# Hash attention with a feed-forward block on one core: the scaled sum of values written into the accumulators' banks ahead of the value products in 11 of 24 halves, banks dealt in the order of making, order remade

## The chip, the core and the metric

The kernel runs on one core of a Trainium2 chip. The metric is the device time of one execution in microseconds; lower is better. Three runs of the kernel before took 295.97, 294.70 and 294.19 us, a median of 294.7 us. Five engines work side by side: PE (matrix products; PEld is its loading of weights), DVE (vector), ACT (scalar, activation functions), POOL, and SP, which issues DMA. Each engine takes its own instructions strictly in the order in which the program writes them and waits for the others by semaphores.

## The reference

`q`, `k` and `v` are 4 batches x 8 heads x 768 tokens x 64, `proj` is 64 x 6, the block is 512 wide with 2048 hidden columns.

```python
q_bits = (einsum('bhsd,dk->bhsk', q, proj) > 0);  k_bits likewise      # 6 bits each
mask   = (bucket of q_bits)[..., :, None] == (bucket of k_bits)[..., None, :]
scores = where(mask, q @ k.T / sqrt(64), -1e9)
attn   = softmax(scores) @ v                        # x = heads side by side, (4, 768, 512)
xn     = (x - mean) / sqrt(var + 1e-6) * g_ln
out    = x + relu(xn @ w_ch1) @ w_ch2
```

A query whose bucket holds no key sees -1e9 everywhere, so that its softmax is uniform and its row is the plain mean of the 768 values. The kernel gets this row by adding 2^-100 times the sum of the values to the numerators, and 2^-100 x 768 to the denominator: beside a single matching key the addend is nothing, without one it is all there is.

## The kernel before

**Units and halves.** The work is cut into 12 units `u` of 256 queries (three to a batch, `u // 3` is the batch), and each unit into two halves `(u, g)` of four heads. A half goes through these steps:

- `S` (L606, PE), six words, one for each block of 128 keys: the scores of four heads, each head in its own 32 rows of the array. Three rounds of products go into the same place: the bucket bits `G` (which push keys of another bucket far down), and the two halves of `q` times `k`.
- `E` (L623, ACT): exp of one score tile of 128 x 1024, from PSUM to bf16 in SBUF. From unit 3 on a half has six tiles in two threes ("trios"): a trio is filled by three `S` words, and emptied by three `E`.
- `A` (L634, PE), six words of eight products: exp tiles times values. `vaug` is the values with a column of ones, so that numerators and denominators (4 heads x 65 columns, for two query tiles: 2 x 260) gather in one accumulator tile `acc` of two banks.
- `na` (L646, DVE): `y = vsB * 2^-100 + acc`, where `vsB` holds, in every partition, the batch's sums of values (made by `su`, `sp` and `sc`, L527 or L525) and in column 64 the constant 768. `acc` is free after it.
- `nb` (L653 to L661, DVE): the reciprocal of the denominators and two products `x = y * rc` that also give the row sums for the norm.

Then the unit's norm (`mn`, `sv`, `rs`, `ce`; POOL, ACT and DVE), a DMA transpose (`fl`), the first feed-forward product and the second. The first product of units 1 to 3 and 11 is plain (`F`, relu `R`, L725, L733, L735). That of units 4 to 10 is made by seven half-size products `M` (L791), whose results are combined out of PSUM by `V` (copy, L800 on ACT or L802 on DVE), `U` (add, L809, DVE), `Q` (relu, L813 or L815) and `ru` (relu, L821 or L823). The second product is made the same way with seven products `P` (L880), combined into `x` by `Y` (L885). `w1s` and `sw` make sums of the weights once, and `tu`, `CA`, `hm`, `bt`, `mw`, `mr`, `cv`, `su` prepare queries, keys, buckets and values of the next batch, all in between.

**PSUM.** Pool `pp` has three places of two banks each. Score tiles and accumulators (and two wide tiles of unit 10) take turns in them; pool `f` has two places of one bank for all else. Which place a tile gets is written in `SLOTS`: the n-th tile made in `pp` takes place `pp[n]`, so the digit decides whose `E` (or `na`) it must wait for.

**Order.** `ORDER` is a list of 1498 words, written out. A word names the step, the engine (t is PE, v DVE, a ACT, p POOL, s SP) and its numbers: `E.a.7.0.1.2` is the exp of half (7, 0), trio 1, tile 2. Every engine executes its words in this order.

Of the kernel before, what the change touches and what calls it, by code (L numbers as in the profile page):

```python
# [10 lines left out]
AOP = mybir.AluOpType  # L11
# [34 lines left out]
A.t.2.1.2.1 na.v.2.1 nb.v.2.1 mw.s.1.1 LX.s.2.0.0 D.t.0.1.0 wg.a.0 ce.v.1.1 fl.s.1.1 ce.v.1.0 fl.s.1.0  # L46
S.t.3.0.0 N.a.3.0.0 sw.v.2.1 cv.a.1.0.2 CA.a.1.1.0 CA.v.1.1.1 S.t.3.0.1 E.a.3.0.0.1 S.t.3.0.2 E.a.3.0.0.0
E.a.3.0.0.2 LX.s.2.0.1 mr.s.1.1.2 mr.s.1.1.0 nc.v.2.1 mr.s.1.1.3 D.t.0.0.2 D.t.0.1.1 D.t.0.1.2 D.t.0.1.3
D.t.0.0.3 tu.v.2.0.0.0 mr.s.1.1.1 sw.v.3.0 ag.v.2.0 tu.v.2.0.0.2 ag.v.2.1 S.t.3.0.3 S.t.3.0.4 Z.v.0.0
N.a.3.0.1 S.t.3.0.5 cv.a.1.0.0 lv.s.1.4.2 Z.v.0.1 E.a.3.0.1.1 F.t.1.1 R.a.1.1 wg.v.2 F.t.1.7 R.v.1.7  # L50
E.a.3.0.1.0 F.t.1.0 E.a.3.0.1.2 rs.p.2 R.a.1.0 lv.s.1.4.1 F.t.1.6 lv.s.2.0.1 lv.s.1.4.0 tu.v.2.0.0.1 ce.v.2.1
S.t.3.1.0 N.a.3.1.0 R.a.1.6 S.t.3.1.1 S.t.3.1.2 ce.v.2.0 w1s.v.1.1 tu.v.2.0.1.1 E.a.3.1.0.2 F.t.1.4
tu.v.2.0.0.3 R.a.1.4 sw.v.2.0 sw.v.1.1 F.t.1.2 A.t.3.0.0.1 R.a.1.2 A.t.3.0.0.2 LX.s.2.1.1 E.a.3.1.0.0 sw.v.4.0
sw.v.1.0 A.t.3.0.1.2 A.t.3.0.1.1 sp.t.1.0 A.t.3.0.0.0 A.t.3.0.1.0 F.t.1.5 E.a.3.1.0.1 cv.a.1.4.0 R.a.1.5
sc.v.1.0 na.v.3.0 su.v.1.4 F.t.1.3 S.t.3.1.3 N.a.3.1.1 S.t.3.1.4 E.a.3.1.1.1 S.t.3.1.5 E.a.3.1.1.0 E.a.3.1.1.2
fl.s.2.1 fl.s.2.0 R.v.1.3 tu.v.2.0.1.3 P.t.1.2 Y.v.1.2 F.t.2.1 R.a.2.1 P.t.1.1 S.t.4.0.0 ss.v.1.1 N.a.4.0.0
S.t.4.0.1 E.a.4.0.0.1 S.t.4.0.2 sw.v.4.1 tu.v.2.0.1.2 O.s.0.2 Y.v.1.1 ss.v.1.2 ss.v.1.4 P.t.1.5 Y.v.1.5
P.t.1.6 cv.a.1.4.2 E.a.4.0.0.2 tu.v.2.0.1.0 ss.v.1.3 CA.a.2.0.1 Y.v.1.6 lv.s.2.0.3 P.t.1.3 lv.s.2.0.0 Y.v.1.3
E.a.4.0.0.0 O.s.0.3 lv.s.2.0.2 lv.s.2.4.2 lv.s.2.4.1 CA.a.2.0.0 A.t.3.1.1.1 A.t.3.1.1.2 w1s.v.2.1 A.t.3.1.1.0
A.t.3.1.0.0 sp.t.1.4 sc.v.1.4 nb.v.3.0 P.t.1.7 A.t.3.1.0.1 A.t.3.1.0.2 Y.v.1.7 na.v.3.1 F.t.2.6 R.v.2.6  # L60
S.t.4.0.3 nb.v.3.1 N.a.4.0.1 S.t.4.0.4 E.a.4.0.1.1 LX.s.2.1.0 S.t.4.0.5 E.a.4.0.1.0 hm.t.2.0 bt.v.2.0 mn.p.3
sv.a.3.1 sv.a.3.0 P.t.1.4 Y.v.1.4 F.t.2.3 R.a.2.3 tu.v.2.1.1.2 su.v.2.0 F.t.2.4 E.a.4.0.1.2 F.t.2.2 rs.p.3
on.p.2 R.a.2.4 w1s.v.4.1 ce.v.3.0 ce.v.3.1 S.t.4.1.0 S.t.4.1.1 N.a.4.1.0 R.a.2.2 S.t.4.1.2 mw.s.2.0 lv.s.2.4.3
lv.s.2.4.0 F.t.2.5 E.a.4.1.0.1 F.t.2.7 R.a.2.5 tu.v.2.1.0.0 tu.v.2.1.0.2 tu.v.2.1.1.3 w1s.v.1.0 tu.v.2.1.1.1
A.t.4.0.0.0 A.t.4.0.1.1 A.t.4.0.1.0 A.t.4.0.1.2 E.a.4.1.0.0 fl.s.3.0 A.t.4.0.0.1 A.t.4.0.0.2 na.v.4.0 F.t.2.0
R.v.2.0 E.a.4.1.0.2 R.a.2.7 S.t.5.0.0 N.a.5.0.0 S.t.5.0.1 E.a.5.0.0.1 cv.a.2.0.0 S.t.5.0.2 E.a.5.0.0.2
ss.v.2.1 ss.v.2.2 E.a.5.0.0.0 P.t.2.2 Y.v.2.2 tu.v.2.1.0.3 P.t.2.1 fl.s.3.1 F.t.3.6 R.a.3.6 Y.v.2.1 P.t.2.6
S.t.4.1.3 N.a.4.1.1 S.t.4.1.4 O.s.0.1 E.a.4.1.1.1 S.t.4.1.5 ss.v.2.4 tu.v.2.1.1.0 P.t.2.5 tu.v.2.1.0.1 Y.v.2.6
ss.v.2.3 Y.v.2.5 P.t.2.7 su.v.2.4 mr.s.2.0.3 O.s.1.1 P.t.2.3 O.s.0.0 O.s.1.0 O.s.1.3 Y.v.2.3 E.a.4.1.1.0
A.t.4.1.1.0 A.t.4.1.0.2 E.a.4.1.1.2 A.t.4.1.0.0 nb.v.4.0 A.t.4.1.1.1 A.t.4.1.1.2 A.t.4.1.0.1 na.v.4.1  # L70
mr.s.2.0.2 Y.v.2.7 F.t.3.1 S.t.5.0.3 S.t.5.0.4 N.a.5.0.1 S.t.5.0.5 R.a.3.1 nb.v.4.1 w1s.v.3.1 mr.s.2.0.1
E.a.5.0.1.2 P.t.2.4 Y.v.2.4 F.t.3.4 E.a.5.0.1.1 E.a.5.0.1.0 CA.v.2.1.1 hm.t.2.1 CA.v.2.1.0 cv.v.2.4.0
w1s.v.3.0 bt.v.2.1 cv.v.2.0.2 R.a.3.4 S.t.5.1.0 N.a.5.1.0 mn.p.4 sv.a.4.1 sv.a.4.0 S.t.5.1.1 S.t.5.1.2 rs.p.4
E.a.5.1.0.2 F.t.3.7 R.a.3.7 LX.s.3.0.1 LX.s.3.0.0 tu.v.3.0.0.2 F.t.3.2 A.t.5.0.1.1 A.t.5.0.0.2 A.t.5.0.0.1
E.a.5.1.0.1 R.a.3.2 tu.v.3.0.1.1 mr.s.2.0.0 A.t.5.0.1.2 A.t.5.0.0.0 ce.v.4.0 fl.s.4.0 tu.v.3.0.1.0
tu.v.3.0.0.1 A.t.5.0.1.0 ce.v.4.1 na.v.5.0 tu.v.3.0.1.3 mw.s.2.1 O.s.1.2 F.t.3.5 R.a.3.5 F.t.3.3 F.t.3.0
tu.v.3.0.0.0 R.v.3.0 E.a.5.1.0.0 tu.v.3.0.0.3 R.a.3.3 S.t.5.1.3 N.a.5.1.1 S.t.5.1.4 E.a.5.1.1.1 ss.v.3.1
S.t.5.1.5 E.a.5.1.1.2 E.a.5.1.1.0 P.t.3.2 Y.v.3.2 fl.s.4.1 w1s.v.2.0 ss.v.3.2 P.t.3.1 lv.s.3.0.0 P.t.3.5
O.s.2.1 Y.v.3.5 Y.v.3.1 S.t.6.0.0 N.a.6.0.0 S.t.6.0.1 cv.a.2.4.2 S.t.6.0.2 E.a.6.0.0.2 E.a.6.0.0.0 P.t.3.6
ss.v.3.4 E.a.6.0.0.1 CA.v.3.0.0 Y.v.3.6 P.t.3.3 mr.s.2.1.0 tu.v.3.0.1.2 ss.v.3.3 nb.v.5.0 Y.v.3.3 CA.a.3.0.1  # L80
A.t.5.1.1.2 A.t.5.1.1.1 A.t.5.1.0.0 A.t.5.1.1.0 A.t.5.1.0.2 A.t.5.1.0.1 P.t.3.7 na.v.5.1 nb.v.5.1 mn.p.5
Y.v.3.7 hm.t.3.0 bt.v.3.0 S.t.6.0.3 N.a.6.0.1 S.t.6.0.4 E.a.6.0.1.1 bs.v.4.1 bs.v.4.3 bs.v.4.2 S.t.6.0.5
mr.s.2.1.3 E.a.6.0.1.2 O.s.2.0 sp.t.2.0 sc.v.2.0 mr.s.2.1.2 LX.s.3.1.0 mr.s.2.1.1 P.t.3.4 Y.v.3.4 M.t.4.1.0
V.v.4.1.0 E.a.6.0.1.0 M.t.4.2.0 U.v.4.1.0 mw.s.3.0 S.t.6.1.0 O.s.3.0 N.a.6.1.0 w1s.v.4.0 M.t.4.6.0 sv.a.5.1
# [77 lines left out]
TYPES = "222222333333333333333333"  # L162

WIDE = {10}
SUMS = 3

SLOTS = dict(
    B="000000",
# [15 lines left out]
    vnat="01010101",  # L184
    vsB="0101",
    vsum="000",
    x="012301320132",
    xnT="010101010101",
)

@with_exitstack
def kernel(
# [16 lines left out]
    P = 128  # L209
# [80 lines left out]
    def vsB(b):  # L290
        return sb(f"vsB{b}", [P, H, D + 1], F32, "vsB", 2)
# [652 lines left out]
```

## Time and profile before

| | |
|---|---|
| median of three runs | 294.7 us |
| the profiled execution: its time, and its span from the first to the last instruction | 293.72 us, 292.0 us |
| PE busy | 280.4 us, 96% of the span, 4924 products |
| DVE busy | 244.8 us, 84%, 587 instructions |
| ACT busy | 228.9 us, 78%, 285 instructions |
| POOL busy | 32.9 us, 11% |
| TensorE clock granted | 1.000 |
| exp `E` on ACT | 144 of 1112 ns |
| `na` on DVE | 24 of 690 ns |

The profile gives for each engine the time in which it executed something. Products on PE are pipelined and their ends are modelled, so "busy" is not "at its peak" there. In a list of groups a row reads: line, engine, operation, tile written <- tiles read, shapes, count | busy us, mean ns of one | idle time of the engine just before them, and what ended it. In a list of waits a row reads: who <- for whom: us in total, times, longest us. Times in a timeline are us from the start of the span.

### The profile page before, as it was taken

What the parts mean: (1) busy time and instruction counts of PE and PEld (TensorE: products, weight loads), DVE (VectorE), ACT (ScalarE), POOL (GpSimd) and SP (SyncE); (2) the same over time, 40 slices, a digit from 0 to 9 for tenths busy, and PEclk for the clock granted to TensorE, in tenths of its full rate; (3) what the DMA queues carried; (4) which work ended last, traced back from release to release, by engine and by line L of the source; (5) the groups of instructions that cost most, each with busy time, mean ns of one, the idle gap of its engine ahead of it and who ended that gap; (6) DMA issues with size and microseconds to landing.
All of it is one profiled execution on the core that took longest, in us unless ns stands there. A gap on an engine that the chain in (4) does not pass through costs nothing.

```text
span 292.0 us, 11314 instructions
## 1 busy us (share of the span) xinstructions
PE 280.4 (96%) x4924; PEld 228.0 (78%) x4927; DVE 244.8 (84%) x587; ACT 228.9 (78%) x285; POOL 32.9 (11%) x83
## 2 busy tenths in 40 slices
PE   8998999999999999999998999899999999999993
PEld 5777767558887886877886878698788789998882
DVE  5758899899998989898997899797997997998552
ACT  4889999999999859879847989898897896664240
POOL 4560500110003002001000102000101011010000
PEclk9999999999999999999999999999999999999999
DMA  6999999268752560444942012500042202003233
GB/s 205 362 293 270 217 278 173 58 203 225 203 159 75 135 225 2 111 146 106 205 140 60 4 38 57 114 11 2 12 101 56 57 3 55 24 0 56 53 93 91
DMA packets 31059, 34.15 MB, mean 117 GB/s; under 512 B 15521, under 2 KB 27809, under 8 KB 31010
## 3 DMA queue, kind: packets, MB, share of 16 engines
q1 hardware_dynamic: 25938, 28.72, 35.4%
q0 software_dynamic: 4224, 4.19, 8.7%
q8 instruction: 38, 0.62, 0.9%
q10 hardware_dynamic: 848, 0.53, 0.7%
q14 instruction: 11, 0.09, 0.1%
HBM read 27.86 MB, written 6.88 MB: 119 GB/s over the span
## 4 chain that ended last, share of the span: by engine, by line
PE 84%; DVE 7%; ACT 6%; issue 1%; DVEq 0%; ACTq 0%
PE sc L606 17%; PE X L880 12%; PE acc L634 11%; PE f L725 10%; PE Ma L791 7%; PE Yb L880 6%; ACT E L623 4%; PE Ya L880 3%; PE Me L791 3%; PE hp L550 3%; PE hf L418 3%; PE f L828 2%; PE Mb L791 2%; PE warm L388 1%; DVE T L329 1%
## 5 line engine op out<-in xcount | busy, mean ns | idle before, releaser
L623 ACT ACTIVATE E<-sc,bias_sb 128x1024 bf16<-128x1024 f32 x144 | 152.2, 1112 | 17.8 <-PE sc L606 17.2
L606 PE MATMUL sc<-qb,kb 32*128 32x256 bf16 x1152 | 52.4, 267 | 0.0
L606 PE MATMUL sc<-G 6*128 6x256 bf16 (+1 forms) x576 | 43.0, 272 | 3.2 <-ACT E L623 3.1
L634 PE MATMUL acc<-vaug,E 128*128 128x65 bf16 x1152 | 43.1, 193 | 0.4 <-ACT E L623 0.4
L634 PEld LDWEIGHTS <-E 128*128 128x128 bf16 x1152 | 40.5, 97 | 2.1 <-issue 1.0
L725 PE MATMUL f<-xnT,w_sb 128*128 128x256 bf16 x320 | 38.8, 273 | 0.4 <-ACT hb L733 0.2
L880 PEld LDWEIGHTS <-hb 128*128 128x128 bf16 x352 | 33.0, 98 | 7.3 <-issue 3.1
L725 PEld LDWEIGHTS <-w_sb 128*128 128x128 bf16 x320 | 30.2, 98 | 5.4 <-issue 2.1
L606 PEld LDWEIGHTS <-kb 32*128 32x128 bf16 x1152 | 30.6, 93 | 1.2
L606 PEld LDWEIGHTS <-G 6*128 6x128 bf16 (+1 forms) x576 | 17.4, 91 | 17.2 <-issue 12.4
L733 ACT ACTIVATE hb<-f 128x512 bf16<-128x512 f32 x33 | 19.6, 599 | 13.5 <-PE f L725 10.5
L880 PEld LDWEIGHTS <-S 128*128 128x128 bf16 x264 | 25.2, 98 | 4.3 <-issue 1.1
L329 DVE STREAM_TRANSPOSE T<-X 128x384 f32<-128x384 f32 (+2 forms) x52 | 26.6, 539 | 0.0
L885 DVE TENSOR_TENSOR x<-X,x 128x256 f32<-128x256 f32 x44 | 18.3, 418 | 5.8 <-PE X L880 5.6
L880 PE MATMUL Yb<-w_sb,S 128*128 128x256 bf16 x176 | 22.8, 273 | 0.0
L791 PEld LDWEIGHTS <-w_sb 128*128 128x128 bf16 x336 | 20.2, 97 | 3.0 <-issue 2.8
L880 PE MATMUL X<-wt,hb 128*128 128x256 bf16 x168 | 21.8, 273 | 0.0
L791 PEld LDWEIGHTS <-Wx 128*128 128x128 bf16 x336 | 19.6, 98 | 2.3 <-issue 2.1
L646 DVE SCALAR_TENSOR_TENSOR y<-vsB,acc 128x520 f32<-128x520 f32 x24 | 16.6, 690 | 5.0 <-PE acc L634 4.8
L669 POOL TENSOR_TENSOR rw<-rw 128x2 f32<-128x2 f32 x9 | 2.1, 237 | 139.1 <-DVE x L659 139.1
L791 PE MATMUL Ma<-bs,Wx 128*128 128x128 bf16 x192 | 14.7, 219 | 0.0
L659 DVE SCALAR_TENSOR_TENSOR x<-y,rc 128x256 f32<-128x256 f32 x36 | 13.9, 422 | 0.6
(134 smaller groups left out, 441.4 us busy)
## 6 DMA issues: line engine op xcount, KB each, us to landing
out_dram<-x SPq DMA_DIRECT2D x45, 128.0 KB
X<-in_k_dram SPq DMA_DIRECT2D x7, 768.0 KB
vn<-in_v_dram SPq DMA_DIRECT2D x24, 192.0 KB
X<-in_q_dram SPq DMA_DIRECT2D x6, 768.0 KB
w_sb<-in_moe_w_ch_dram POOLq DMA_DIRECT2D x8, 512.0 KB, 12.5
vn<-in_v_dram SPq DMA_DIRECT2D x2, 768.0 KB
X<-in_q_dram SPq DMA_DIRECT2D x2, 512.0 KB
Bd<-B SPq DMA_DIRECT2D x6, 96.0 KB
```

The source lines that it names most:

```text
L329: nc.vector.transpose(d[:, j], s[:, j, kj0 : kj0 + n])
L418: nc.tensor.matmul(hf(g, t, kp)[:, :256], pfull[:, j], tp(g, t, kp)[:, j], start=(j == 0), stop=(j == 1))
L606: m = nc.tensor.matmul(sc(u, g, a, p)[:, bank, 256 * half : 256 * half + 256], lh, rh, start=(rep == 0), stop=(rep == 2), skip_group_check ...
L623: nc.scalar.activation(Ep(u, g, a, p), sc(u, g, a, p), AF.Exp, scale=EXP_SCALE, bias=bias_sb)
L634: nc.tensor.matmul(acc[:, qt, (D + 1) * i : (D + 1) * (i + 1)], Ep(u, g, a, p)[:, bank, 256 * half + P * qt : 256 * half + P * qt + P], va ...
L646: nc.vector.scalar_tensor_tensor(yt(u, g), vs, EPS_ROW, made[f"acc{u}_{g}"][:, :, :A], op0=AOP.mult, op1=AOP.add,)
L659: nc.vector.scalar_tensor_tensor(xo[:, t], a[:, t, :, 0:D], 1.0, rc[:, t].to_broadcast([P, 4, D]), op0=AOP.mult, op1=AOP.mult, accum_out=r ...
L725: nc.tensor.matmul(f1[:, n].rearrange("p (t x) -> p t x", t=2), w1_sb[:, dt, P * nt : P * nt + P], xnT(u)[:, :, dt], start=(dt == 0), stop ...
L733: nc.scalar.activation(hb(u)[:, 2 * p : 2 * p + 2], f1, AF.Relu)
L791: nc.tensor.matmul(m[:, n], lh(kt)[:, P * nt : P * nt + P], rh[:, kt], start=(first and n == 0 and kt == 0), stop=(kt == 1), skip_group_ch ...
L880: nc.tensor.matmul(f2, lh[:, n], rh[:, n], start=(first and n == 0), stop=(n == 7), skip_group_check=True)
L885: nc.vector.tensor_tensor(x, made[f"{prod(u, k)}{u}"], x, op=AOP.add)
```

## The change

Three things are changed together.

1. In 11 halves, (4,0), (4,1), (5,0), (5,1), (7,1), (8,1), (9,0), (10,0), (10,1), (11,0) and (11,1), a new step `pa` copies the scaled sum of values into the accumulator's two banks before the first `A` of the half; all 48 value products then add to it. `na` is gone there, and `nb` reads numerators and denominators straight from `acc` in PSUM instead of from `y`. Nine `pa` stand on ACT, two (unit 11) on DVE. The set `LATE` names the 13 halves that keep `na`. So that nothing need be scaled at that point, `vsB` is scaled by 2^-100 when it is made, for batches 1 to 3 (`sc`, `on`). The score products now open each bank once (`opened`), where each 256 columns opened it before.
2. The places in `pp`, `f`, `E`, `X` and `x` are dealt anew, in the order in which the tiles are made. In `pp`, of the 128 tiles made from unit 3 on, 119 took the place that stands first in `ORDER` to be freed; now 125 do.
3. `ORDER` is remade from its 300th word on (PE is changed from its 112th word on). It has the same number of words. Besides `na` and `pa`, 47 words change their engine between ACT and DVE.

```diff
-A.t.2.1.2.1 na.v.2.1 nb.v.2.1 mw.s.1.1 LX.s.2.0.0 D.t.0.1.0 wg.a.0 ce.v.1.1 fl.s.1.1 ce.v.1.0 fl.s.1.0
+A.t.2.1.2.1 na.v.2.1 nb.v.2.1 mw.s.1.1 D.t.0.0.2 D.t.0.1.0 wg.a.0 cv.a.1.0.0 lv.s.1.4.0 LX.s.2.0.0 S.t.3.0.0
...
+LATE = {(u, g) for u in range(3) for g in range(2)} | set([(3, 0), (3, 1), (6, 0), (6, 1), (9, 1), (7, 0), (8, 0)])
...
-    pp="012120212021102012012012010120120201021021021012021002010212102012102121012011022021210021010201201020120102102120102101200210201210202110210212012021120101201201202102021",
+    pp="012120212021102012012012010120120201021021021012021001202102102012102121020121202102021210201210210212012102120120101202010210102012021012010212102021201210212012100210120",
...
     def on(eng, b):
         nc.gpsimd.memset(vaug(b)[:, :, :, D : D + 1], 1.0)
-        nc.gpsimd.memset(vsB(b)[:, :, D : D + 1], float(S))
+        nc.gpsimd.memset(vsB(b)[:, :, D : D + 1], float(S) * (EPS_ROW if b else 1.0))
...
     def scp(eng, b, hs):
...
+        elif eng is nc.scalar:
+            nc.scalar.activation(dst, src, AF.Copy, scale=EPS_ROW)
+        else:
+            eng.tensor_scalar(dst, src, EPS_ROW, None, op0=AOP.mult)
...
+                fresh = (u, g, a, p, bank) not in opened
+                opened.add((u, g, a, p, bank))
                 m = nc.tensor.matmul(
                     sc(u, g, a, p)[:, bank, 256 * half : 256 * half + 256], lh, rh,
-                    start=(rep == 0), stop=(rep == 2), skip_group_check=True,
+                    start=fresh, stop=(rep == 2), skip_group_check=True,
                 )
...
+    def pa(eng, u, g):
+        acc = ps(f"acc{u}_{g}", [P, 2, 512], "pp")[:, :, :A]
+        vs = vsB(u // 3)[:, 4 * g : 4 * g + 4].rearrange("p h e -> p (h e)").unsqueeze(1).to_broadcast([P, 2, A])
+        if eng is nc.scalar:
+            nc.scalar.copy(acc, vs)
+        else:
+            eng.tensor_copy(acc, vs)
...
-        first, last = begun[u, g] == 1, begun[u, g] == 6
+        first, last = begun[u, g] == 1 and (u, g) in LATE, begun[u, g] == 6
...
-            yt(u, g), vs, EPS_ROW, made[f"acc{u}_{g}"][:, :, :A], op0=AOP.mult, op1=AOP.add,
+            yt(u, g), vs, 1.0 if u > 2 else EPS_ROW, made[f"acc{u}_{g}"][:, :, :A], op0=AOP.mult, op1=AOP.add,
...
-        a = yt(u, g).rearrange("p t (h e) -> p t h e", e=D + 1)
+        a = (yt(u, g) if (u, g) in LATE else made[f"acc{u}_{g}"][:, :, :A]).rearrange("p t (h e) -> p t h e", e=D + 1)
```

Two places show how the order moves. The first is ACT's queue from the second trio of half (8,1) to the next three exp of half (9,0); the names are the tile with its unit, half, trio and place in the trio (`E8_111` is half (8,1), trio 1, tile 1), `hb6` is the hidden layer of unit 6, `V651` a copy for its `U`. Before:

```order
L623 ACTIVATE E8_111_4509<-sc8_111_4446,bias_sb_66 128x1024
L623 ACTIVATE E8_110_4512<-sc8_110_4457,bias_sb_66 128x1024
L623 ACTIVATE E8_112_4522<-sc8_112_4443,bias_sb_66 128x1024
L813 ACTIVATE hb6_4425<-Ma60_4334 128x4x128
L623 ACTIVATE E9_000_4564<-sc9_000_4524,bias_sb_66 128x1024
L623 ACTIVATE E9_002_4581<-sc9_002_4551,bias_sb_66 128x1024
L800 COPY V651_4631<-Me61_4622 128x512
L623 ACTIVATE E9_001_4641<-sc9_001_4527,bias_sb_66 128x1024
```

Now, with the copy into `acc8_1` (`pa`, L638) among them:

```order
L630 ACTIVATE E8_111_4493<-sc8_111_4436,bias_sb_66 128x1024
L630 ACTIVATE E8_112_4495<-sc8_112_4447,bias_sb_66 128x1024
L630 ACTIVATE E8_110_4499<-sc8_110_4433,bias_sb_66 128x1024
L828 ACTIVATE hb6_4414<-Ma60_4352 128x4x128
L630 ACTIVATE E9_001_4559<-sc9_001_4512,bias_sb_66 128x1024
L638 COPY acc8_1_4561<-vsB2_2649 128x2x260
L630 ACTIVATE E9_002_4587<-sc9_002_4509,bias_sb_66 128x1024
L815 COPY V651_4616<-Me61_4607 128x512
L630 ACTIVATE E9_000_4661<-sc9_000_4536,bias_sb_66 128x1024
```

The three exp of half (8,1) come in another order, and so do those of (9,0). The first `S` word of half (9,0) fills tiles `sc9_000` and `sc9_001` before; by the digits of `pp` they took the places of `sc8_112` (the third of the three exp above) and of `sc8_110` (the second). Now the first `S` word fills `sc9_002` and `sc9_001`, in the places of `sc8_111` and `sc8_112`, the first and the second exp. The same holds at half (7,1): its first `S` word took the places of the third and second exp of the trio before it, `E7_010` and `E7_012`; now it takes those of the first and second, `E7_011` and `E7_010`. At both places one or two `M` stand on PE between this `S` word and the next one, which needs the third.

The second place is DVE's queue around the end of half (8,1): `acc8_1` is its accumulator, `rc81` the reciprocals, `hb6`, `S61`, `bs7` and `x6` belong to the feed-forward parts of units 6 and 7. Before:

```order
L646 SCALAR_TENSOR_TENSOR y81_4685<-vsB2_2195,acc8_1_4603 128x520
L809 TENSOR_TENSOR hb6_4425<-Me61_4622,V661_4620 128x4x128
L823 TENSOR_SCALAR hb6_4425<-hb6_4425 128x8x128 x2
L865 TENSOR_TENSOR S61_4698<-hb6_4425 128x1024
L767 TENSOR_TENSOR bs7_4737<-xnT7_4578 128x256
L885 TENSOR_TENSOR x6_3606<-Ya6_4753,x6_3606 128x256
```

Now:

```order
L838 TENSOR_SCALAR hb6_4414<-hb6_4414 128x8x128
L668 RECIPROCAL rc81_4694<-acc8_1_4561 128x8
L674 SCALAR_TENSOR_TENSOR x8_4421,rw8_4422<-acc8_1_4561,rc81_4694 128x256 x2
L824 TENSOR_TENSOR hb6_4414<-Me61_4607,V661_4605 128x4x128
L838 TENSOR_SCALAR hb6_4414<-hb6_4414 128x8x128
L880 TENSOR_TENSOR S61_4700<-hb6_4414 128x1024
L900 TENSOR_TENSOR x6_3646<-Ya6_4744,x6_3646 128x256
```

Before, one instruction freed the accumulator, and the reciprocal and the two products of this half came twelve rows later, after most of the `Y` of unit 6. Now these three free the accumulator, and stand ahead of the `U`, `ru` and first sum that unit 6 still needs.

More of the change, by code (lines that the diff above doesn't have):

```diff
@@ L50 @@
[L50 to L64, printed above, removed]
@@ L70 @@
[L70 to L84, printed above, removed]
@@ L186 @@
     vsum="000",
-    x="012301320132",
+    x="012301230123",
     xnT="010101010101",
```

208 lines of the change are left out of this document (119 added, 89 removed).

## The prediction

> **What bounds the kernel now.** I read the busy times first, then stretches of the time line, then the waits, and last the two places where PE stood still longest.
>
> ```profile
> span 292.0 us, 11314 instructions
> PE 280.4 (96%) x4924; PEld 228.0 (78%) x4927; DVE 244.8 (84%) x587; ACT 228.9 (78%) x285; POOL 32.9 (11%) x83
> PE 84%; DVE 7%; ACT 6%; issue 1%; DVEq 0%; ACTq 0%
> ```
>
> PE is busy for 96% of the span and carries 84% of the chain that ended last. The change neither removes nor adds a product: PE has 4924 before and after. So only PE's standing still can be won, and only lengthening it can lose. The changed part of PE's program begins at 57.9 us and the last product ends at 287.4 us; I cut that time where the fifth unit's second half ends its first trio (113 us) and where unit 9 begins (186 us). Columns: length, then busy us of PE, PEld, DVE, ACT, POOL, each with its instructions, the clock, the DMA share and GB/s.
>
> ```profile
> 57.90:113.00 55.10, 54.99 (x873) 42.47 (x875) 50.35 (x113) 48.97 (x59) 4.20 (x10) 1.00 0.58 164
> 113.00:186.00 73.00, 71.33 (x1364) 58.32 (x1361) 65.91 (x155) 60.43 (x78) 5.76 (x16) 1.00 0.37 92
> 186.00:248.00 62.00, 60.69 (x1180) 52.33 (x1176) 52.62 (x125) 51.67 (x66) 4.41 (x12) 1.00 0.18 42
> 248.00:287.40 39.40, 39.09 (x504) 35.26 (x500) 29.90 (x72) 17.58 (x29) 1.40 (x4) 1.00 0.19 44
> sum 229.50, PE 226.09 PEld 188.37 DVE 198.78 ACT 178.65 POOL 15.76; mean PE 56.52 PEld 47.09 DVE 49.69 ACT 44.66 POOL 3.94
> ```
>
> Over these 229.5 us PE stands still for 229.50 - 226.09 = 3.4 us, and 1.7 us of that lies in the stretch from 113 to 186. Visible idle time is therefore a small prize. DVE has 55.10 - 50.35 = 4.8 us left in the first stretch, 7.1 in the second, 9.4 in the third. Whom PE waited for in these 229.5 us:
>
> ```profile
> PE sc L606 <- ACT E L623: 2.4, 2, 1.3
> PE acc L634 <- ACT E L623: 0.3, 1, 0.3
> ACT E L623 <- PE sc L606: 14.0, 25, 1.7
> DVE y L646 <- PE acc L634: 2.9, 5, 1.2
> ```
>
> Two waits of score products for an exp make 2.4 of the 3.4 us. In the other direction ACT waits 14.0 us for scores, 25 times: ACT is seldom late. PE's and ACT's rows at the two places, 155 and 185 us:
>
> ```profile
> 156.10 0.61 PE L791 MATMUL Me<-bs,Wx 128*128 128x128 bf16 x8
> 157.97 0.29 PE L606 MATMUL sc<-G 6*128 6x256 bf16 x4 [1.27 <-ACT E L623]
> 154.80 3.12 ACT L623 ACTIVATE E<-sc,bias_sb 128x1024 bf16<-128x1024 f32 x3 [0.20 <-PE sc L606]
> 185.73 0.61 PE L791 MATMUL Ma<-bs,w_sb 128*128 128x128 bf16 x8
> 187.43 0.29 PE L606 MATMUL sc<-G 6*128 6x256 bf16 x4 [1.09 <-ACT E L623]
> 229.43 0.63 PE L606 MATMUL sc<-G 6*128 6x256 bf16 x4
> 184.25 3.12 ACT L623 ACTIVATE E<-sc,bias_sb 128x1024 bf16<-128x1024 f32 x3 [0.22 <-PE sc L606]
> ```
>
> Both times three exp run in a row, and PE goes on only behind the third: 154.80 + 3.12 = 157.92, then 157.97. The reader is to see which exp it is. The waiting word is the first `S` of (7,1), and of (9,0); its two tiles had the banks of the third and of the second exp. At 229.43 us, the first `S` of (11,0), where the banks were those of the first and second, no wait is seen, only 0.63 us in place of 0.29 for the four products.
>
> **The change, part by part.** *Banks.* At these two places the first `S` word now gets the banks of the first and second exp. It can go on one exp earlier, 3.12 / 3 = 1.04 us, and the third exp is needed only by a later `S`, with one or two `M` ahead of it. Of 1.27 and 1.09 us that wins 1.0 each, **-2.0 us**; the bounds are 0 (something else is late) and -2.4.
>
> *Work moved.* The rows that give the durations:
>
> ```profile
> L646 DVE SCALAR_TENSOR_TENSOR y<-vsB,acc 128x520 f32<-128x520 f32 x24 | 16.6, 690 | 5.0 <-PE acc L634 4.8
> L659 DVE SCALAR_TENSOR_TENSOR x<-y,rc 128x256 f32<-128x256 f32 x36 | 13.9, 422 | 0.6
> L653 DVE RECIPROCAL rc<-y 128x8 f32<-128x8 f32 x24 | 4.7, 194 | 0.3
> L885 DVE TENSOR_TENSOR x<-X,x 128x256 f32<-128x256 f32 x44 | 18.3, 418 | 5.8 <-PE X L880 5.6
> L733 ACT ACTIVATE hb<-f 128x512 bf16<-128x512 f32 x33 | 19.6, 599 | 13.5 <-PE f L725 10.5 <-PE sc L606 2.9
> L477 ACT ACTIVATE w_sb<-w_sb,gT 128x512 bf16<-128x512 bf16 x4 | 2.5, 716 | 0.0
> L802 DVE COPY V<-Ma 128x512 f32<-128x512 f32 x11 | 7.6, 689 | 2.4 <-PE Ma L791 2.4
> L498 ACT CAST vaug<-vn 128x768 bf16<-128x768 f32 x10 | 8.3, 833 | 1.0 <-DMA G<-Bd 0.6 <-PE sc L606 0.4
> L500 DVE CAST vaug<-vn 128x768 bf16<-128x768 f32 x3 | 1.7, 554 | 0.0
> L336 ACT ACTIVATE kb<-T 128x1536 bf16<-128x1536 f32 x3 | 4.5, 1486 | 0.0
> L340 DVE CAST kb<-T 128x1536 bf16<-128x1536 f32 x3 | 2.9, 951 | 0.0
> L821 ACT ACTIVATE hb<-hb 128x1024 bf16<-128x1024 bf16 x6 | 6.3, 1056 | 0.8 <-DVE hb L809 0.4 <-PE sc L606 0.4
> L823 DVE TENSOR_SCALAR hb<-hb 128x1024 bf16<-128x1024 bf16 x15 | 6.1, 422 | 0.2
> L754 DVE TENSOR_TENSOR Wx<-w_sb 128x1024 bf16<-128x1024 bf16 x4 | 2.7, 676 | 0.0
> L693 DVE TENSOR_SCALAR xc<-x,rw,rs 128x512 bf16<-128x512 f32 x18 | 9.4, 533 | 0.4 <-POOL rs L702 0.4
> L329 DVE STREAM_TRANSPOSE T<-X 128x384 f32<-128x384 f32 x44 | 23.4, 556 | 0.0
> ```
>
> DVE loses 11 `na`, 11 x 0.690 = 7.6 us. It gains two `pa` (1.4 at 0.69), a net four evictions of 128x512 (`V`, `R`, `Q`: 4 x 0.689 = 2.8), a net two `CA`, the casts of `q` and `k` (three come, one goes: 2 x 0.951 = 1.9), four casts of values (2.2) and one relu (0.4), and gives up two copies of 128x256 (0.8). The sum is -7.6 + 1.4 + 2.8 + 1.9 + 2.2 + 0.4 - 0.8 = **+0.3 us**: DVE's load stays.
>
> ACT gains nine `pa`. None is in the trace, and none reads SBUF and writes PSUM. The bounds by the nearest 512-wide rows are 599 ns (from PSUM) and 716 ns (inside SBUF); I take 650 ns, between them, 5.9 us in all. It loses a net four evictions (4 x 0.60 = 2.4), two `CA` (3.0), four casts (3.3) and one relu (1.1), and gains the two small copies, under 0.6 each. That is about **-3 us** on an engine with 14 us of waiting: it pays nothing by itself, but lets exp be on time. By the Trainium skill, "ScalarE: Activation LUTs", section "Step-by-step: what each stage is for", an activation that writes to PSUM is the faster one; by that sentence the nine copies would cost 599 ns or less, 5.4 us, which changes the total by nothing, since ACT's 3 us have no price.
>
> *Where DVE's work lies.* Between the same two marks, 113 and 186 us, DVE's words change: three `na` and a `CA` net in (-2.1 + 1.0), three evictions more (2.1), two casts of values (1.1), one `nb` more (0.194 + 2 x 0.422 = 1.0), two weight sums `w1s` (1.4), less one norm product and one transpose (1.1). That is **+3.4 us** in the stretch, and as much less outside it. DVE would be busy 65.9 + 3.4 = 69.3 of 73 us. What it costs is bounded by 0 (all goes into the 7.1 us in which DVE waits) and +3.4 (none does). In the stretch before, DVE was at 91% and PE stood still for 0.1 us, so that load at this level costs next to nothing; I take **+0.5**.
>
> *The accumulator's release.* `acc` was free one instruction after the last `A` (0.690 us); now after the reciprocal and two products, 1.04 us. `nb` reads PSUM now. The row with one operand in PSUM (`x<-X,x`, 418 ns) and the row from SBUF alone (422 ns) agree, so I count no extra. The Trainium skill speaks against that: "Perfetto Trace Analysis", section "Optimizing Scalar/DVE Operations", has about 125 ns of access for DVE on PSUM and 60 on SBUF; by it 33 instructions would add an estimated 2.1 us to DVE. The two rows of this trace show no such step. The bank comes 0.35 us later in 11 halves; at three, (4,1), (8,1) and (9,0), only one `S` word stands on PE between `nb` and the `S` that takes the bank. The bounds are 0 and 11 x 0.35 = 3.9; I take a third of 3 x 0.35, **+0.3**. Behind `nb` on DVE wait a `U` and a `Y`, for whose banks PE's next `M` and `P` wait.
>
> *The copy ahead of A.* The first `A` now waits for `pa` on ACT, behind whose exp it stands. At seven of the eleven, PE has other products between the two words; at (7,1), (10,0), (10,1) and (11,1) none. Bounds 0 and 4 x 0.65 = 2.6 us; I take 0, since ACT has 3 us less to do and waited 14.0 us for PE. If that cover goes, the 2.6 us are the price.
>
> *DMA.* SP's words are remade too. The share of the DMA engines in use is 0.58, 0.37, 0.18 and 0.19 in the four stretches, and of the casts of values ACT waited 0.6 us for one (row L498); I price this at 0, and a load that comes late at the 1 to 2 us that a queue of `CA` and casts on DVE behind it would be worth (0.951 + 0.554 each).
>
> **Sum.** -2.0 + 0.5 + 0.3 + 0 = -1.2 us. The profiled execution took 293.72 us (span 292.0), so it would take 292.5. The median of the three runs, 294.7, is 1.0 above it; so the predicted median is **293.5 us**.
>
> **Rivals.** *DVE becomes the bound of the middle (slower).* DVE must now run `nb` when the products end, in front of the `U`, `ru` and `Y` that hold PSUM banks; it can no longer put it off by twelve rows, as in (8,1). If its 7.1 us of idle time in the stretch are waits for PE that cannot be filled, the 3.4 us of more work lengthen the stretch, and the bank waits, which lie in it, win nothing: 294.7 + 3.4 = **298.1 us**. It decides from DVE busy over 95% of the stretch on; 69.3 of 73 is 95%. For it: `x<-X` makes DVE wait 5.6 us for PE, idle time that a shift does not fill. Against it: the first stretch. The longer PSUM access of the skill would make this likelier by its 2.1 us.
>
> *The waits only move.* The third exp, or `pa`, is late where the first was; ACT needs 3.12 us for a trio whatever the banks. Then the gain is 0 and the time **294.7 us**. Against it: 229.43 us, above.
>
> *All of PE's visible idle time goes (faster).* With ACT 3 us lighter, all 3.4 us vanish: 294.7 - 3.4 = **291.3 us**. Against it: 1.0 us lies in waits that no part of the change addresses.
>
> **How the numbers follow.** A measurement of this kernel (its three runs spread by 0.6%) tells a change from none at about 1%, 2.9 us. Forecast 0.38, moved waits 0.22, both within 1%; DVE-bound 0.25, slower by over 1%; all idle time gone 0.15, faster by over 1%. So faster 0.15, within 1% 0.60, slower 0.25. The range takes in the third and just reaches the DVE case: **291.2 to 298.2**, leaving out the outer parts of the last two, under 2 in 10.
>
> **What would show it.** Right: PE's waits for exp, 2.4 us in two, are gone; DVE idle time from unit 5 to unit 9 falls to about 4 us with PE's idle time there under 1.5; `pa` takes 0.6 to 0.72 us on ACT; `nb` takes 0.2 + 2 x 0.42. Wrong: a wait of `acc` for a copy of ACT, or of score products for `nb`, of more than 1 us in all; the two products of `nb` near 490 ns; PE standing still for more than 5 us in the changed part.

## The result, and the profile after

The changed kernel takes **291.83 us** (median of 13 runs, 291.22 to 293.78) beside 294.19 us for the kernel before (13 runs on the same chip): a ratio of 0.9926, with a 95% interval from 0.9902 to 0.9951. That is 2.4 us less by the two medians and 2.2 us less by the ratio, where 1.2 us less were forecast. It lies within 1%, as predicted. Medians in this document are of all executions; the ratios leave out three slow ones, one of 550.1 us of `after_dve5` and two of `before_pa`.

From the page of the kernel after: the span, the busy times, the granted clock in 40 slices, and the shares of the chain that ended last.

```profile
span 292.0 us, 11313 instructions
PE 283.6 (97%) x4927; PEld 228.4 (78%) x4927; DVE 245.2 (84%) x587; ACT 225.9 (77%) x285; POOL 33.0 (11%) x83
PEclk9999799999999999999999999999999999999998
PE 84%; DVE 10%; ACT 3%; issue 1%; POOL 1%; DVEq 0%; ACTq 0%
```

The loads are as forecast: DVE +0.4 us (forecast +0.3), ACT -3.0 (about -3); DVE's share of the chain is 10% in place of 7. The 4927 products beside 4924 are no change: the trace of the kernel before lacks three products of unit 0 (L828 has 29 beside 32 loads of weights), and every later trace of this program's order has 4927. The span is no shorter than before because the unchanged first part took 2.2 us longer in this one execution, the slowest of the 13: its mean granted clock was 0.83 between 30 and 40 us (the 7 in the row of the clock). So the two traces are compared from the first `A` of half (2,1) on, which both programs reach with the same work behind them; from there to the last product the granted clock is 1.00 in both. PE's first and last rows in that stretch and DVE's last row, before:

```profile
56.14 1.63 PE L634 MATMUL acc<-vaug,E 128*128 128x65 bf16 x48
286.34 1.04 PE L880 MATMUL Yc<-wt,hb 128*128 128x256 bf16 x8
287.42 0.42 DVE L885 TENSOR_TENSOR x<-Yc,x 128x256 f32<-128x256 f32 x1
```

And after:

```profile
58.36 1.62 PE L649 MATMUL acc<-vaug,E 128*128 128x65 bf16 x48
287.04 1.04 PE L895 MATMUL Yc<-wt,hb 128*128 128x256 bf16 x8
288.12 0.42 DVE L900 TENSOR_TENSOR x<-Yc,x 128x256 f32<-128x256 f32 x1
```

From that `A` to the end of the last product: 287.38 - 56.14 = 231.24 us before, 288.08 - 58.36 = 229.72 after, **-1.52**. From the last `Y` to the end of the span: 292.0 - 287.84 = 4.2 before, 292.0 - 288.54 = 3.5 after, **-0.65** with the traces' third digits. Together -2.2, the gain that the ratio shows; and 0.65 of it lies behind the last product, where the prediction had put nothing.

The stretches of the kernel after that answer to the four of before (PE's order differs, so each is cut where PE has as many products ahead of it as before, to within eight; columns as there):

```profile
60.12:114.83 54.71, 54.58 (x867) 41.56 (x866) 51.05 (x113) 43.62 (x58) 3.63 (x11) 1.00 0.56 151
114.83:186.70 71.87, 71.53 (x1361) 58.53 (x1362) 67.13 (x160) 61.63 (x76) 6.07 (x16) 1.00 0.38 103
186.70:248.57 61.87, 61.52 (x1185) 52.19 (x1183) 51.47 (x122) 51.53 (x68) 4.54 (x12) 1.00 0.20 41
248.57:288.10 39.53, 39.21 (x506) 34.99 (x502) 29.79 (x70) 18.78 (x30) 1.64 (x4) 1.00 0.28 49
sum 227.98, PE 226.85 PEld 187.27 DVE 199.44 ACT 175.57 POOL 15.88; mean PE 56.71 PEld 46.82 DVE 49.86 ACT 43.89 POOL 3.97
```

PE stands still for 227.98 - 226.85 = 1.1 us there, 3.4 before. In the second stretch it is 0.3 us (1.7 before), and DVE has 4.7 us left (7.1 before). Of the two bank waits only that at (7,1) lies in the second stretch; the one at (9,0), from 186.34 to 187.43 us, lies behind the mark of 186 (the DVE-bound rival has both in the second), and the third stretch's idle time fell from 1.3 to 0.35 us with it. PE's waits for exp over the whole run, before and after:

```profile
PE sc L606 <- ACT E L623: 3.1, 5, 1.3
PE sc L613 <- ACT E L630: 0.8, 3, 0.3
```

The two of 1.3 and 1.1 us are gone. Other waits of the kernel after, from the first `A` of (2,1) on:

```profile
ACT E L630 <- PE sc L613: 18.9, 22, 2.4
DVE rc L668 <- PE acc L649: 2.0, 5, 0.6
PE Me L806 <- DVE V L817: 0.3, 1, 0.3
```

ACT waits for scores 18.9 us in place of 14.0, as it has 3 us less to do; DVE waits 2.0 us for the last `A` with its reciprocal. PE has no wait for a copy into the accumulator and none of scores for `nb`.

The place at (9,0) in the kernel after, ACT's row and PE's:

```profile
185.08 3.12 ACT L630 ACTIVATE E<-sc,bias_sb 128x1024 bf16<-128x1024 f32 x3
186.96 0.57 PE L613 MATMUL sc<-G 6*128 6x256 bf16 x4
```

The three exp end at about 186.1, 187.2 and 188.2 us. The score products go on at 186.96, on the banks of the first and second, a good microsecond ahead of the third exp's end. Before, they went on only behind it.

### The profile page after: what moved, and what is told of

It is laid out like the page before. It is cut to its first block, busy times and chain, and to the rows that moved or that the text cites. A ratio compares the mean times of both kernels' runs of the same rounds, so it can differ in the third digit from the quotient of the medians.

```text
span 292.0 us, 11313 instructions
## 1 busy us (share of the span) xinstructions
PE 283.6 (97%) x4927; PEld 228.4 (78%) x4927; DVE 245.2 (84%) x587; ACT 225.9 (77%) x285; POOL 33.0 (11%) x83
## 3 DMA queue, kind: packets, MB, share of 16 engines
q0 software_dynamic: 4224, 4.19, 8.7%
## 4 chain that ended last, share of the span: by engine, by line
PE 84%; DVE 10%; ACT 3%; issue 1%; POOL 1%; DVEq 0%; ACTq 0%
PE sc L613 17%; PE X L895 12%; PE acc L649 11%; PE f L740 10%; PE Ma L806 7%; PE Yb L895 7%; PE Me L806 4%; PE hf L419 3%; PE Ya L895 3%; PE f L843 2%; PE hp L553 2%; PE Mb L806 2%; ACT E L630 2%; DVE T L330 2%; DVE hb L824 2%
## 5 line engine op out<-in xcount | busy, mean ns | idle before, releaser
L613 PE MATMUL sc<-qb,kb 32*128 32x256 bf16 x1152 | 53.4, 270 | 0.0
L613 PE MATMUL sc<-G 6*128 6x256 bf16 (+1 forms) x576 | 43.6, 275 | 0.8 <-ACT E L630 0.8
L740 PE MATMUL f<-xnT,w_sb 128*128 128x256 bf16 x320 | 39.8, 276 | 0.4 <-ACT hb L748 0.2
L748 ACT ACTIVATE hb<-f 128x512 bf16<-128x512 f32 x30 | 17.8, 598 | 12.9 <-PE f L740 10.1
L689 ACT ACTIVATE xc<-x,rw 128x512 bf16<-128x512 f32 x18 | 13.0, 724 | 0.9 <-POOL rw L685 0.5
L880 DVE TENSOR_TENSOR S<-hb 128x1024 bf16<-128x1024 bf16 (+1 forms) x12 | 7.7, 646 | 5.7 <-ACT hb L748 5.2
```

What stands on the lines that cost most here:

```text
L613: m = nc.tensor.matmul(sc(u, g, a, p)[:, bank, 256 * half : 256 * half + 256], lh, rh, start=fresh, stop=(rep == 2), skip_group_check=True,)
L689: nc.scalar.activation(xc(u)[:, t], xt(u)[:, t], AF.Square, bias=r[:, 3, t : t + 1], accum_out=r[:, 4, t : t + 1],)
L740: nc.tensor.matmul(f1[:, n].rearrange("p (t x) -> p t x", t=2), w1_sb[:, dt, P * nt : P * nt + P], xnT(u)[:, :, dt], start=(dt == 0), stop ...
L748: nc.scalar.activation(hb(u)[:, 2 * p : 2 * p + 2], f1, AF.Relu)
L880: eng.tensor_tensor(Ss(u, out)[:, r], in0[:, r], in1[:, r], op=op)
```

## The experiments

One table for all. "PE" is the time in the profiled execution from the start of the first `A` of (2,1) to the end of the last product, "end" that from the end of the last `Y` to the end of the span. In runs that agree in program over a stretch the times of PE repeat to about 0.01 us, which is why small terms can be read from them and not from the medians; the end repeats less well (4.15 to 4.19 us, 3.37 to 3.50). The granted clock is 1.00 over the time of PE in every kernel but before_pa. Each ratio is to the kernel before on the same chip; differences in the text are of the times of PE, unless they are said to be others.

| kernel | median us | ratio to before, 95% interval | PE | end |
|---|---|---|---|---|
| before | 294.1 to 294.8 | | 231.24 | 4.15 |
| after | 291.83 | 0.9926 (0.9902 to 0.9951) | 229.72 | 3.50 |
| before_banks | 291.94 | 0.9921 (0.9902 to 0.9941) | 229.24 | 4.19 |
| before_tail | 293.78 | 0.9987 (0.9971 to 1.0002) | 231.25 | 3.80 |
| before_banks_tail | 291.39 | 0.9919 (0.9893 to 0.9946) | 229.24 | 3.83 |
| before_banks_end | 291.81 | 0.9904 (0.9872 to 0.9936) | 229.25 | 3.80 |
| before_first | 292.39 | 0.9937 (0.9918 to 0.9957) | 229.24 | 3.96 |
| after_banks_back | 293.65 | 0.9987 (0.9973 to 1.0002) | 232.03 | 3.39 |
| before_pa | 322.94 | 1.1005 (1.0946 to 1.1063) | 256.69 | 4.19 |
| after_pa_late | 296.68 | 1.0096 (1.0078 to 1.0115) | 235.28 | 3.40 |
| after_all_late | 297.16 | 1.0095 (1.0059 to 1.0131) | 234.91 | 3.37 |
| after_engines | 309.18 | 1.0491 (1.0455 to 1.0527) | 247.15 | 3.38 |
| after_dve5 | 293.30 | 0.9962 (0.9941 to 0.9984) | 231.41 | 3.37 |
| after_nb_late | 292.63 | 0.9941 (0.9916 to 0.9965) | 230.50 | 3.38 |

**The two bank places alone**, in the kernel before: from the first `S` of (7,1) to the first `S` of (9,0), places 1 and 2 change names (the string's digits from the 106th tile on, over 20 tiles):

```diff
-    pp="...20120 102102120102101200210 2012..."
+    pp="...20120 201201210201202100120 2012..."
```

> The kernel before, with nothing changed but the places in the pool of score tiles: from the first S of (7,1) up to the first S of (9,0) places 1 and 2 change names, so that at both of these words the first two tiles take the banks of the first and second exp and the third tile that of the third exp; who follows whom is the same everywhere else. Theory A (the exp waits were real cost): 2.0 us less than before, 0.7%, and PE's waits of score products for exp fall from 2.4 us to about 0.4. Rival B (the waits only move; another word is late in their place): no change within 0.3 us, and the idle time turns up at the third tile's word or at the M behind it.

Theory A holds, to the hundredth: PE's time falls from 231.24 to 229.24. By stretches between the first `S` words of the units, 0.99 us goes between units 7 and 8, and 1.00 between units 8 and 10 (1.15 up to the first `S` of unit 9, which itself waits no more, and 0.15 back behind it); no other stretch moves by more than 0.01. The rows that show it, of this kernel (whole run, then the timeline):

```profile
PE sc L606 <- ACT E L623: 0.8, 3, 0.3
```

```profile
55.81 1.62 PE L634 MATMUL acc<-vaug,E 128*128 128x65 bf16 x48
284.01 1.04 PE L880 MATMUL Yc<-wt,hb 128*128 128x256 bf16 x8
```

**The same undone in the changed kernel**: the same exchange of digits there.

> The changed kernel, with the two bank places undone: at the first S of (7,1) and of (9,0) the two tiles take the banks of the third and second exp again; all else as changed. Theory A: about 2 us are lost again, 1.0 at each place, so 293.8 us, and PE shows two waits for exp of about 1 us. Rival E (the new order or the lighter ACT makes exp early enough, and the banks no longer matter): 291.8 us as the changed kernel, with no wait of over 0.4 us for exp.

```profile
157.41 0.29 PE L613 MATMUL sc<-G 6*128 6x256 bf16 x4 [1.28 <-ACT E L630]
187.15 0.29 PE L613 MATMUL sc<-G 6*128 6x256 bf16 x4 [1.23 <-ACT E L630]
```

Theory A again: both waits come back, PE's time grows by 2.30 us, and the gain over the kernel before is gone (0.9987). The new order and the lighter ACT don't make exp early enough by themselves.

**One rule for all places**, in the kernel before: from unit 3 on each tile takes the place that is read out first, so 128 of 128 in place of 119. The store that the next part tells of is moved too.

> The kernel before with the place of every tile of the score pool, from unit 3 on, dealt by one rule: the place whose last tile is read first in the order of the words; and with the store of unit 9 ahead of that of unit 11. It has the two bank places among them. Theory A (only these two places were waited for): 291.4 us, as with the two places and the store alone. Otherwise (the five other places cost too): up to 0.8 us less, the waits for exp that are left, 290.6.

PE's time is 229.24 us, as with the two words alone. The other tiles that stood against the rule cost nothing: PE came there late enough anyway.

**The end.** One store moved on SP, in the kernel before:

```diff
-O.s.9.3 O.s.11.0.0 O.s.9.2 Y.v.11.7.1.0 P.t.11.4 ...
+O.s.9.3 O.s.9.2 O.s.11.0.0 Y.v.11.7.1.0 P.t.11.4 ...
```

> The kernel before, with one word moved on SP: the store of a quarter of unit 9 goes ahead of the first store of unit 11 in place of behind it, so that only stores of unit 11 are left at the end. The stretch from the last product's end to the end of the span was 4.6 us before and 3.9 us after the change. Theory C (that store fills the DMA engines when the last ones want them): 0.7 us less, 0.2%, and the last stretch falls to about 3.9 us. Rival D (the end has a fixed length that varies by chance): no change.

SP's queue at the end of the kernel before, and of this one:

```profile
286.74 0.84 SPq L899 DMA_DIRECT2D out_dram<-x  x1
287.68 1.20 SPq L897 DMA_DIRECT2D out_dram<-x  x2
```

```profile
286.25 2.30 SPq L897 DMA_DIRECT2D out_dram<-x  x3
```

Before, the store of 128 KB of unit 9 (L899) takes SP's turn among the last four, and the last is issued 0.5 us later (in the trace 0.51 us behind the last `Y` in place of 0.03). Moved, it gives 0.35 us of the 0.65 (3.80 and 3.83 us in the two kernels that have the move alone or with the two places; 3.96, a gain of 0.2, in before_first). Its ratio alone can't be told from 1.

> Both edits of the two runs above together in the kernel before. If theories A and C both hold: 2.7 us less than before, as much as the whole change won (2.4 us), with none of its copies, none of its new order. If only A holds 2.0 less, if only C 0.7 less, if neither no change.

291.39 us: with two places exchanged over 20 tiles and one moved word the kernel before is as fast as the changed one (0.9919 beside 0.9926). The whole of the new order, with its copies, isn't needed for that time. No kernel of the study beats it by more than the intervals.

> The kernel before with the two bank places changed, and with its last 29 words in the order of the changed kernel (stores of units 9 and 10 ahead of those of unit 11, sums and Y of unit 11 in another order; no copies, no other new order). If what the change won lies in the banks (2.2 us) and in the end (0.75 us by the time from the last product to the end, of which the move of one store gave 0.3): 291.2 us, 2.9 less than before, and 0.6 less than the changed kernel. If the end's length does not follow from its order: 291.9, as with the banks alone.

The end stays at 3.80 us with all of the last 29 words in the new order; the remaining 0.3 us by which the changed kernel's end is shorter isn't in them (see the last section).

**The copies alone**, in the order of before. In 11 halves, as here in (10,0):

```diff
+pa.a.10.0
 A.t.10.0.0.0 A.t.10.0.0.2
 ...
-na.v.10.0 nb.v.10.0
+nb.v.10.0
```

> The copies alone: the kernel before with its order, engines and bank places, and only the first part of the change put in. In the 11 halves the copy into the accumulator stands directly ahead of the first A (nine on ACT, two on DVE), the three instructions of nb stand where na stood, na is gone. DVE gets 6.2 us less to do (11 x 0.69 less 2 x 0.69), ACT 5.4 us more (9 x 0.60), and nothing is taken off ACT for it. Theory F (PE is the bound, and neither the copy ahead of A nor the later release of the bank is waited for): within 0.5 us of before, 294.1. Theory G (the first A waits for the copy, which stands behind exp): up to 2.6 us more, seen as waits of A for the copy of ACT; the later release: up to 3.9 us more, seen as waits of score products for DVE.

25 us more on PE: both theories' numbers are far off. The waits say where; those of PE below are 20.1 us:

```profile
PE acc L649 <- ACT acc L638: 13.4, 8, 3.5
DVE x L674 <- DMA out_dram<-x: 6.3, 2, 3.4
PE sc L613 <- DVE x L674: 4.6, 3, 3.2
PE acc L649 <- DVE acc L640: 2.1, 2, 1.7
```

The longest wait for a copy on ACT and on PE:

```profile
135.75 3.12 ACT L630 ACTIVATE E<-sc,bias_sb 128x1024 bf16<-128x1024 f32 x3
138.75 1.49 ACT L337 ACTIVATE kb<-T 128x1536 bf16<-128x1536 f32 x1
140.12 0.61 ACT L638 COPY acc<-vsB 128x520 f32<-128x520 f32 x1
```

```profile
140.78 1.62 PE L649 MATMUL acc<-vaug,E 128*128 128x65 bf16 x48 [3.51 <-ACT acc L638]
```

The copy itself takes 0.61 us, but it stands behind three exp and a cast of keys, and PE pays for that queue. The longest wait for the release, on DVE and PE of the same kernel:

```profile
101.68 0.42 DVE L674 SCALAR_TENSOR_TENSOR x<-acc,rc 128x256 f32<-128x256 f32 x1 [3.38 <-DMA out_dram<-x]
```

```profile
102.51 0.40 PE L613 MATMUL sc<-G 6*128 6x256 bf16 x4 [3.21 <-DVE x L674]
```

`nb` writes into a place of `x` that a store of an earlier unit still reads. While `na` freed the bank, that did not matter to PE; once `nb` frees it, PE's scores wait for a DMA. A part of the 25 us is the clock: in this execution it was granted at half from 101.5 to 108.3 us, which can have cost up to 3.4 us. It fell while PE stood still in this wait. Whether the wait brought that about isn't shown: two others as long (3.51 and 3.19 us) weren't followed by a lower clock. The granted clock over this run:

```profile
PEclk9999999999998699999999999999999999999999
```

**The copies moved** to directly ahead of the first `A`, in the changed kernel:

```diff
-pa.a.9.0 bs.v.7.2 Y.v.6.6 P.t.6.7 Y.v.6.3 E.a.9.1.0.0 sv.a.8.0 O.s.5.1 A.t.9.0...
+bs.v.7.2 Y.v.6.6 P.t.6.7 Y.v.6.3 E.a.9.1.0.0 sv.a.8.0 O.s.5.1 pa.a.9.0 A.t.9.0...
```

> The changed kernel with the eleven copies moved to directly ahead of the first A of their half, on the same engine; at (7,1), (10,0) and (10,1) they stand there already. On ACT that puts the copies of (5,1), (8,1), (9,0) and (11,1) behind one or two exp, that of (9,0) also behind a squares word, that of (5,0) behind a relu. Theory J (what cost 25 us where the copies were put into the old order is that they stand behind exp on ACT, so that A waits for them): A waits for copies again, 1 us each or more at these places, and 5 us or more are lost. Theory K (it was the late release of the bank, or the load): no more than 1 us.

```profile
PE acc L649 <- ACT acc L638: 4.1, 4, 1.5
PE acc L649 <- DVE acc L640: 0.7, 1, 0.7
```

Theory J: the load is the same, only eight copies stand a few words later, and 5.55 us are lost. In the queue of its own engine a copy passes anything at five places only: one or two words of ACT at (5,0), (5,1), (8,1) and (9,0), and one of DVE at (11,0). (The expectation puts the copy of (11,1) on ACT; it stands on DVE, and passes nothing there.) The loss lies there: 1.70 us between units 6 and 7, for example, and 2.57 between 9 and 10. So in this order it is the copy's place in its queue that decides. For the 25 us above that goes for the 15.5 us of waits for copies; the later release (4.6 us) and the clock are in them as well.

**The copies taken out** of the changed kernel (`pa.a.10.0` goes, `na.v.10.0` comes back ahead of `nb.v.10.0`, and so in 11 halves):

> The changed kernel without the copies: in the 11 halves the copy is taken out and na is put back, directly ahead of nb, everything else (order, engines, bank places) as changed. DVE gets 6.2 us more, ACT 5.4 us less; in the stretch from 115 to 187 us four halves are concerned, so DVE gets 2.8 us more there, from 67.9 of 72.7 us to 70.7, 97%. Theory F (DVE's load costs nothing as long as PE has other products to do): within 0.5 us of the changed kernel, 291.8. Theory H (DVE is the bound of the middle from 95% on): 2.8 us more, 294.6, with PE waiting for DVE there.

```profile
PE Ma L806 <- DVE hb L824: 1.2, 4, 0.4
PE f L740 <- DVE x L900: 0.7, 2, 0.6
PE Yb L895 <- DVE x L900: 0.7, 3, 0.3
```

5.19 us more, for 5.9 us more of DVE (251.1 beside 245.2). Theory F falls; theory H named the right engine but too small a place: 1.6 of the 5.2 us are lost in the stretch that it speaks of. No single wait carries it: it is many of 0.2 to 0.6 us, most of them for DVE's `U` and `Y`, from unit 5 on.

**The engines put back** (47 letters, such as `Q.v.5.0` to `Q.a.5.0`), in the changed kernel:

> The changed kernel with the 47 words that changed between ACT and DVE put back on their engine of before, in the new order. ACT gets about 8 us more (it then has 5.4 us more than before, for the copies), DVE about 6 us less. Theory F: within 0.5 us of the changed kernel, since PE waits for neither. Theory I (it was the lighter ACT that made exp be on time): the waits of score products for exp come back, over 1 us of them, and the time is 1 to 2 us more, 293 to 294.

```profile
PE Yb L895 <- DVE x L900: 2.7, 3, 2.4
PE sc L613 <- ACT E L630: 2.6, 6, 0.7
PE f L740 <- ACT hb L748: 1.7, 3, 0.9
PE Me L806 <- ACT V L815: 1.4, 1, 1.4
```

17.4 us more. Exp is late again, as theory I says, but that is 2.6 us (0.8 in the changed kernel) of it; the rest is spread over relus, copies and combinations that come late on one or the other engine, and one load (1.2 us). ACT has 74.4 us without work in that run, 24%.

**More work on DVE** in the second stretch of the changed kernel, five words `dx.v` spread evenly:

```diff
+    def dx(eng):
+        nc.vector.bn_stats(sb("dx", [P, 6], F32, "dx", 1), w2_sb[:, 0, :])
```

> The changed kernel with five more instructions on DVE, spread evenly over its words from the keys of batch 2 to the first S of (9,0), the stretch that the third term of the prediction speaks of. Each takes statistics of 512 weights that nothing uses, about 0.5 us (its row will tell), so some 2.5 to 3 us in all; nothing waits for them but what stands behind them on DVE. Theory F, as the prediction has it (0.5 of 3.4): 0.4 us more. Theory H, which putting na back in the changed kernel speaks for (5.2 us of time for 6.2 us of DVE): nearly all of it, 2 to 3 us more.

```profile
L635 DVE BATCH_NORM_STATS2 dx<-w_sb x5: 650/680/686, 119.9 to 179.2; 128x6 f32<-128x512 bf16 x5
```

```profile
113.36:186.92 73.56, 72.10 (x1360) 58.56 (x1361) 69.84 (x165) 61.91 (x76) 5.89 (x16) 1.00 0.38 101
```

The stretch grows from 71.87 to 73.56 us, by 1.69 for 5 x 0.68 = 3.4 us: half of it. Neither theory has that number, and it is no rate: with the copies taken out, 5.9 us more of DVE cost 5.19.

**A later release** at (4,1), (8,1) and (9,0): one `dx.v` directly ahead of `nb`.

> The changed kernel with one extra instruction on DVE (statistics of 512 weights that nothing uses, about 0.5 us) directly ahead of nb at (4,1), (8,1) and (9,0), so that these three accumulators are released that much later; they are the halves where one S word stands between. Theory L, as the prediction has it (a third of the delay at these three): 0.5 us more. Theory M (PE stands still for each delay): 1.5 us, with waits of score products for DVE. Theory N (other products cover it): nothing, except what DVE's load costs.

0.78 us more for 3 x 0.68 = 2.0 us, 0.38 of the delay. One wait of scores for `nb` is seen, 0.4 us:

```profile
PE sc L613 <- DVE x L678: 0.4, 1, 0.4
PE Ma L810 <- DVE hb L828: 0.4, 2, 0.2
```

That is near theory L's share, but DVE's load is in it as well, so that it bounds the release and doesn't measure it alone.

## Why the prediction was right, and where it was off

The direction was right, and the mechanism of the main term. The predicted time was 1.7 us too high. The forecast change was -1.2 and the measured one -2.4 by the medians; and its base, the median of three runs, was 0.5 above that of 13.

- **Banks, -2.0 us.** Right, in place, size and sign: 1.00 at each of the two words with nothing else changed, and 2.30 when taken away from the changed kernel, inside the bounds of 0 and -2.4. The rival that the waits only move has fallen with it.
- **DMA, 0.** The step that failed. "I price this at 0" looked at the share of the DMA engines up to the last product, and not at what comes behind it. The end is 0.65 us shorter. 0.35 of it is one store of unit 9 that SP issued among those of unit 11, so that the last store came 0.5 us later; the order of SP's words showed that beforehand. The other 0.3 is a step in SP's closing waits whose cause is open.
- **Where DVE's work lies, +0.5.** The sum hides two wrong factors. DVE's work in the stretch grew by 67.13 - 65.91 = 1.2 us, not by 3.4, since words between two marks on PE aren't the instructions that DVE executes between them. And the price taken from the first stretch (91% busy, no idle time of PE, so "next to nothing") is wrong: 3.4 us cost 1.7. Half of 1.2 is 0.6, near the 0.5 by luck. The mark of 113 us, too, is where (5,1) begins its first trio, not where it ends it.
- **The accumulator's release, +0.3.** Not refuted. No wait of scores for `nb` is seen after, and 2.0 us of delay cost at most 0.78, about the third that was taken. The 0.5 us by which the changed kernel's PE time stands above that with the banks alone (229.72 and 229.24) is this, DVE and the new order together, +0.8 in the forecast; the runs don't part them.
- **The copy ahead of A, 0.** Right for the kernel as it was made: no wait for a copy is seen. But its bound, 2.6 us, counted only the copy's own 0.65 us, at four halves. With copies one or two words later in their queues it was 5.55 us, and in the old order the waits for copies alone were 15.5. The price of a step on an in-order queue is what stands ahead of it.
- **Work moved, no price.** Right in the sum, wrong in the reason. DVE and ACT have 16% and 23% of idle time, and the prediction took ACT's waiting for PE as cover. Putting back the engines costs 17.4 us, taking out the copies 5.2. The engine moves and the copies pay for each other: the copies take 6.3 us off DVE, and the moves put 5.4 us back on it from ACT (the durations of what DVE executes, added up, with each and without). Together they are no gain against the kernel before with its banks and its store put right, and either without the other is a loss.
- **The DVE-bound rival.** Its threshold (from 95% on everything shows) isn't what was seen: at 69.84 of 73.56 us, just under 95%, half of the added work showed. **All idle time gone**, 291.3 us: the nearest number of all, but of PE's 3.4 us of idle time only the two bank waits' part went, and the end brought the rest.

The durations, in the kernel after:

```profile
L638 ACT COPY acc<-vsB x9: 596/597/604, 95.7 to 233.0; 128x520 f32<-128x520 f32 x9
L668 DVE RECIPROCAL rc<-y x13: 159/195/204, 24.1 to 219.6; 128x8 f32<-128x8 f32 x13
L668 DVE RECIPROCAL rc<-acc x11: 202/207/208, 99.0 to 254.5; 128x8 f32<-128x8 f32 x11
L674 DVE SCALAR_TENSOR_TENSOR x<-acc,rc x22: 419/422/426, 99.2 to 255.1; 128x256 f32<-128x256 f32 x22
L674 DVE SCALAR_TENSOR_TENSOR x<-y,rc x14: 418/423/427, 81.5 to 220.2; 128x256 f32<-128x256 f32 x14
```

`pa` takes 0.597 us, at the lower bound of 0.599; the estimate of 0.65 was high, and the sentence of the Trainium skill, "ScalarE: Activation LUTs", section "Step-by-step: what each stage is for", that an activation into PSUM is the faster one, gave the better number. No row here writes the same copy to SBUF, so the sentence itself isn't tested. `nb` takes 0.21 + 2 x 0.42 us from PSUM, and 0.19 + 2 x 0.42 from SBUF. The Trainium skill, "Perfetto Trace Analysis", section "Optimizing Scalar/DVE Operations", has about 125 ns of access for DVE on PSUM and 60 on SBUF, by which one would estimate 65 ns more for each instruction. That isn't seen: 0 ns more in the products and 12 in the reciprocal.

## What to carry to other kernels

Where tiles take turns in a few banks, look first at which reader of the trio the waiting word got: two such words were worth 2.0 us here. The rest of a rewritten order of 1,200 words gave nothing that the medians show: PE's time is 0.5 us longer with it, and the end 0.3 us shorter. Idle time on an engine (16% of DVE and 23% of ACT here) is not slack that can be given away on an in-order queue; what a new instruction costs is the queue ahead of it, and it has to be placed before it is priced. And price the end of the program, behind the last product, as a stretch of its own.

## What was not expected of the hardware

- Between the same two words on PE the time repeats to 0.01 us from one execution to another, and with other stretches changed (229.24, 229.24, 229.25, 229.24 in four kernels), while the unchanged part ahead of it took between 55.8 and 58.4 us over all fourteen traces. The longest of these had a granted clock of 0.83 between 30 and 40 us. So in these executions the scatter arises mainly ahead of 60 us; before_pa, with half the clock from 101.5 us on, is the exception.
- SP closes the program with a row of waits for the DMAs. One of them comes 0.40 us behind the one ahead of it in all seven kernels with the order of before (0.401 to 0.408), and 0.06 us in all seven with the new order (0.061 to 0.062), whatever the stores. That is the 0.34 us of the end that no word moved here explains: the last 29 words of the new order, put into the kernel before, leave it at 0.40. Its cause is open.
- More work on a busy DVE cost neither nothing nor all of its time: half (1.69 of 3.4 us) in a stretch where DVE was 93% busy, and 0.88 of it (5.19 of 5.9 us) over the whole run, 84% busy, with the copies taken out.
